# Block 2 in half products, batch 3's attention one block earlier, and the sums and squares moved with them

## The chip, the cores and the metric

The kernel runs on one NeuronCore of one Trainium2 chip. The metric is the device time of one execution in microseconds (us). Its engines are TensorE (PE), VectorE (DVE), ScalarE (ACT), GpSimd (POOL) and SyncE (SP), whose queue here issues the transposing DMAs and the stores.

## The reference

```python
kv  = einsum('bhsd,bhse->bhde', k, v)          # q, k, v: [8, 8, 576, 64] fp32
o   = einsum('bhsd,bhde->bhse', q, kv)
att = o / sqrt(mean(o*o, -1) + 1e-6) * g_norm
x   = att.transpose(0, 2, 1, 3).reshape(4608, 512)
ffn = (gelu(x @ w_gate) * (x @ w_val)) @ w_out   # 512 -> 1536 -> 512
out = x + sigmoid(x @ w_res) * ffn
```

## The kernel before

A block is the 512 first tokens of one batch (blocks 0 to 7). The 64 last tokens of the eight batches together make block 8. TensorE runs, for each block: 12 slices of gate and value products (512 columns each), four gate products `rps`, then the product with w_out as seven products of half size instead of eight. In some blocks the gate and value products, too, are done as half products: a *group* of four slices takes 2 x 7 x 4 matmuls of 256 columns in place of 2 x 4 x 4 of 512. They need sums of weights and of tokens, made by DVE.

The attention of a later batch is woven into the block's slots, one slot being one slice or one step of the products. Each batch needs: q brought to token order by copies (`by_token`), a DMA transpose `d_qT`, the k-v product (`a_kv`), the o product (`a_o`, which reads qT), squares on ACT and reductions on DVE (`a_ss`), a normalisation of about a dozen tiny operations (`a_norm`), the scaled result t (`a_t`), its multiplication by g (`a_x`), and a DMA transpose `d_xT` for the matmuls. The program puts each engine's work into its queue in this order, so a slot number is a place in five queues.

Names in the trace lines: `gps` and `vps` are a slice's gate and value products, `hid` is DVE's product of the two (it frees their banks of PSUM), `op` the o product, `rps` the four gate products with w_res, `wA`, `wD`, `wE` and `wF` the banks of the seven products with w_out. The *F sum* is DVE's addition that makes `wF`, which a later product needs, and the *half sums* are sums of `hid` for these products. `osb` holds the block's result; a *residual addition* is POOL's addition of x (`t`) to it.

```python
    def plan_attn(b):                  # batches 2 and 3
        ...
        if b == 2:
            at(m, 0, lambda: by_token(b))
            at(m, 1, *begin)           # begin: attn_begin, d_qT, last tokens' transpose
            k0, o0, n0 = 4, 6, 9
        else:
            if b == 3:
                aside_out(m - 1, "22", lambda: by_token(b), *begin)
            ...
            k0, o0, n0 = 1, 3, 7
        at(m, k0, lambda: a_kv(b))
        ...
        at(m, NF, lambda: d_xT(b, 0, NJ))
        ...
    GROUPS = {blk: (1, 2) for blk in range(3, B - 1)} | {B - 1: (1, 0, 2), B: (0, 1, 2)}
    ...
    def plan_attn_ahead(b):            # batches 4 to 7, two blocks ahead
        ...
        else:                          # m, the block it runs in, is not in GROUPS
            at(m, 5, lambda: by_token(b, act, slice(0, 2)))
            at(m, 6, lambda: by_token(b, act, slice(2, 4)))
            at(m, 7, *begin)
            at(m, NF - 1, lambda: a_kv(b, act))
            at(m, NF, lambda: load_behind(b, b - 1))
        ...
        at(m, NF, lambda: a_o(b), lambda: a_ss(b, 0), lambda: a_ss(b, 1))
        aside_out(m, "D", lambda: a_ss(b, 2), lambda: a_ss(b, 3))
        aside_out(m, "gates", *[lambda: a_ss(b, NJ)] * rem, lambda: a_norm(b, 0, NJ + rem, pool))
```

## Time and profile before

| | before |
|---|---|
| time, median of runs (lowest to highest) | 333.25 us (333.08 to 333.75) |
| span of the profiled run, granted clock | 331.3 us, 0.995 |
| PE, DVE, ACT, POOL busy | 97%, 78%, 56%, 40% |
| blocks 1, 2, 3, 4 | 35.91, 37.24, 35.19, 33.45 us |
| blocks 5, 6, 7 | 34.46, 32.12, 30.96 us |

A block's length is the start of its first gate matmul in the TensorE timeline taken from that of the next block. The share of busy time hides the stages: with TensorE at 97%, what counts is which block has a gap, and whose work ends it. The lines are shown in the prediction.

### The profile page before, as it was taken

To read this page: it belongs to the slowest core of one execution; us is meant where nothing else is said; L and a number is where in the kernel's file an instruction comes from. 1 tells how busy PE (TensorE), PEld (TensorE's weight loads), DVE (VectorE), ACT (ScalarE), POOL (GpSimd) and SP (SyncE) were. 2 spreads that over 40 slices of the span, in tenths; PEclk is the share of its full clock that TensorE was granted. 3 is DMA by queue.
4 is the path that set the end of the run, shared out by engine and by line. 5 is a ranking of instruction groups with operands and counts; after the bars stand their busy time and mean duration, and the time that the engine had idled before them with its cause. 6 is when DMAs were issued, how large, how long until landed. Compare 5 with 4: busy or idle time off the path is not lost.

```text
span 331.3 us, 7035 instructions
## 1 busy us (share of the span) xinstructions
PE 320.6 (97%) x2768; PEld 219.6 (66%) x2768; DVE 258.7 (78%) x482; ACT 184.6 (56%) x334; POOL 133.9 (40%) x196
## 2 busy tenths in 40 slices
PE   8899999999999999899999999999999999999993
PEld 3554454445844476686768686868587888788882
DVE  6856769579867996869786987697979977687754
ACT  3763474374338381667466746675465466646660
POOL 2882152980055038418641864114611241151232
PEclk9999999999999999999999999999999999999997
DMA  8999999679579749976937593800340030011004
GB/s 256 318 205 203 195 203 177 161 120 136 85 126 202 156 72 162 223 110 77 141 137 136 66 150 129 143 4 0 129 79 3 0 129 3 0 64 64 2 0 127
DMA packets 76690, 38.85 MB, mean 117 GB/s; under 512 B 42098, under 2 KB 74354, under 8 KB 76658
## 3 DMA queue, kind: packets, MB, share of 16 engines
q0 software_dynamic: 38752, 17.17, 41.3%
q1 hardware_dynamic: 37328, 20.71, 24.3%
q10 hardware_dynamic: 578, 0.52, 0.5%
q8 instruction: 21, 0.34, 0.4%
q14 instruction: 11, 0.09, 0.1%
HBM read 38.80 MB, written 9.44 MB: 146 GB/s over the span
## 4 chain that ended last, share of the span: by engine, by line
PE 88%; DVE 4%; DMA 3%; SPq 1%; ACT 1%; issue 1%; POOL 0%; DVEq 0%; ACTq 0%
PE vps L361 13%; PE gps L361 13%; PE rps L381 10%; PE wA L456 9%; PE Av L698 8%; PE Ag L698 7%; PE Fv L698 4%; PE Fg L698 4%; PE fps L398 3%; PE w L456 2%; PE wD L456 2%; PE wF L456 2%; PE wE L456 2%; PE Ev L698 2%; PE Eg L698 2%; PE kvp L208 2%
## 5 line engine op out<-in xcount | busy, mean ns | idle before, releaser
L349 ACT ACTIVATE ge<-gps 128x512 f16<-128x512 f32 x52 | 30.8, 597 | 64.6 <-PE gps L361 64.3
L361 PE MATMUL vps<-xT,wv 128*128 128x512 f16 x200 | 51.3, 379 | 0.9 <-DVE hid L350 0.9
L361 PE MATMUL gps<-xT,wg 128*128 128x512 f16 x200 | 51.4, 379 | 0.3 <-DMA xT<-t 0.3
L350 DVE TENSOR_TENSOR hid<-ge,vps 128x512 f16<-128x512 f16 x52 | 35.4, 683 | 20.0 <-PE vps L361 17.5
L698 PEld LDWEIGHTS <-ws 128*128 128x128 f16 x448 | 43.6, 98 | 5.6 <-issue 0.5
L735 POOL TENSOR_TENSOR hid<-ge,c 128x512 f16<-128x512 f16 x14 | 16.3, 1163 | 73.1 <-ACT ge L729 73.1
L456 PEld LDWEIGHTS <-hid_s 128*128 128x128 f16 x384 | 37.5, 98 | 6.1 <-issue 1.7
L498 POOL TENSOR_TENSOR osb<-osb,t 128x512 f32<-128x512 f32 x28 | 32.0, 1168 | 23.0 <-DVE osb L494 22.7
L361 PEld LDWEIGHTS <-wv 128*128 128x128 f16 x200 | 19.6, 98 | 24.6 <-issue 1.1
L361 PEld LDWEIGHTS <-wg 128*128 128x128 f16 x200 | 19.0, 98 | 21.8 <-DMA xT<-t 0.6
L381 PE MATMUL rps<-wr,xT 128*128 128x512 f16 x144 | 33.3, 380 | 0.0
L456 PEld LDWEIGHTS <-hid 128*128 128x128 f16 x288 | 28.1, 98 | 5.4 <-issue 0.4
L390 ACT ACTIVATE th<-rps 128x512 f32<-128x512 f32 x36 | 21.5, 598 | 12.2 <-PE rps L381 12.2
L381 PEld LDWEIGHTS <-xT 128*128 128x128 f16 x144 | 13.5, 98 | 14.8
L719 DVE TENSOR_TENSOR Fg<-Ag,d 128x512 f32<-128x512 f32 x14 | 9.8, 700 | 16.2 <-PE Ag L698 9.0
L245 DVE TENSOR_REDUCE ss<-sq 128x8 f32<-128x512 f32 x32 | 20.6, 678 | 2.3 <-ACT sq L243 1.9
L456 PE MATMUL wA<-wo_ts,hid_s 128*128 128x256 f16 x168 | 20.6, 272 | 1.0 <-DVE wF L429 1.0
L307 DVE TENSOR_TENSOR t<-op,ny 128x512 f16<-128x512 f32 x28 | 18.2, 684 | 2.8 <-POOL ny L287 2.7
L395 ACT ACTIVATE th<-th 128x512 f32<-128x512 f32 x36 | 19.9, 625 | 0.0
L698 PEld LDWEIGHTS <-wg 128*128 128x128 f16 x168 | 16.4, 98 | 2.7
L698 PEld LDWEIGHTS <-wv 128*128 128x128 f16 x168 | 16.4, 98 | 1.9
L698 PE MATMUL Ag<-ts,ws 128*128 128x256 f16 x112 | 16.8, 273 | 0.0
(183 smaller groups left out, 649.5 us busy)
## 6 DMA issues: line engine op xcount, KB each, us to landing
out_dram<-osb SPq DMA_DIRECT2D x14, 512.0 KB, 2.7
qraw<-in_q_dram POOLq DMA_DIRECT2D x7, 512.0 KB, 6.7
k<-in_k_dram POOLq DMA_DIRECT2D x7, 512.0 KB, 8.4
v<-in_v_dram POOLq DMA_DIRECT2D x7, 512.0 KB, 11.4
wg<-in_moe_w_gate_dram POOLq DMA_DIRECT2D x2, 512.0 KB, 8.1
wv<-in_moe_w_val_dram POOLq DMA_DIRECT2D x2, 512.0 KB, 8.7
wo<-in_moe_w_out_dram POOLq DMA_DIRECT2D x2, 512.0 KB, 13.8
out_dram<-osb SPq DMA_DIRECT2D x4, 256.0 KB, 2.7
```

Source lines behind the costliest of these rows:

```text
L245: nc.vector.tensor_reduce(out=out_, in_=sq, op=ALU.add, axis=mybir.AxisListType.X)
L307: nc.vector.tensor_tensor(out=t, in0=o, in1=scale, op=ALU.mult)
L349: nc.scalar.activation(out=ge, in_=gps, func=AF.Gelu)
L350: nc.vector.tensor_tensor(out=hids[blk][:, f, :], in0=ge, in1=vps, op=ALU.mult)
L361: nc.tensor.matmul(ps[:, j0 * P : j1 * P], lhsT=w[:, cc, :], rhs=xT_t[blk][:, j0:j1, cc, :], start=(cc == 0 and j0 == 0), stop=(cc == NP - ...
L381: nc.tensor.matmul(rps, lhsT=xT_t[blk][:, j, cc, :], rhs=wr16[:, cc, :], start=(cc == 0), stop=(cc == NP - 1),)
L390: nc.scalar.activation(out=th, in_=rps, func=AF.Tanh, scale=0.5)
L395: nc.scalar.activation(out=th, in_=th, func=AF.Copy, scale=0.5, bias=0.5)
L456: nc.tensor.matmul(ps[:, e - es[0], :], lhsT=a[:, f, e * P : (e + 1) * P], rhs=b[:, f, :], start=(start and e == es[0] and f == 0), stop=( ...
L498: nc.gpsimd.tensor_tensor(out=res_all[of], in0=res_all[of], in1=t_t[blk][of], op=ALU.add)
L698: nc.tensor.matmul(out_[:, r, :], lhsT=lhsT, rhs=rhs, start=(first and r == 0 and c == 0), stop=(c == 1), skip_group_check=True,)
L735: eng.tensor_tensor(out=dst, in0=ge[q], in1=source(q, "v"), op=ALU.mult)
```

## The change

Its intent: half products in block 2 save TensorE time. They are affordable only if batch 3's attention leaves block 2, so it moves to block 1. Block 1's DVE and POOL work is rearranged to make room.

```diff
+    def plan_attn_2():
+        b, m = 2, 1
+        act = nc.scalar.copy
+        at(m - 1, 2 * NF + 3, lambda: by_token(b, act, slice(0, 2)))
+        at(m, 0, lambda: by_token(b, act, slice(2, 4)), lambda: attn_begin(b), lambda: d_qT(b))
+        at(m, 2, lambda: a_kv(b))
+        at(m, 3, lambda: load_behind(b))
+        at(m, 1, lambda: wo_sums(1))          # all sums of w_out on DVE now
+        at(m, 3, lambda: wo_sums(3))
+        at(m, 4, lambda: a_o(b))
         ...
+        at(m, 6, lambda: a_norm(b, 0, NJ))
+        for j in range(NJ):
+            at(m, 7 + j // 2, lambda j=j: a_t(b, j))
+            at(m, 8 + j // 2, lambda j=j: a_x(b, j))
+        at(m, 9, lambda: d_xT(b, 0, NJ))
-    GROUPS = {blk: (1, 2) for blk in range(3, B - 1)} | ...
+    GROUPS = {blk: (1, 2) for blk in range(2, B - 1)} | ...
     # plan_attn_ahead, now for batches 3 to 7; block 1 is the only one not in GROUPS
-            at(m, 5, lambda: by_token(b, act, slice(0, 2)))
-            at(m, 6, lambda: by_token(b, act, slice(2, 4)))
-            at(m, 7, *begin)
+            at(m, 9, lambda: by_token(b, act, slice(0, 2)))
+            at(m, 10, lambda: by_token(b, act, slice(2, 4)), *begin)
-            at_word(m, 1, "h21", lambda: a_rem_o(b))
-        at(m, NF, lambda: a_o(b), lambda: a_ss(b, 0), lambda: a_ss(b, 1))
+            at_word(m, 1, "h21", lambda: a_rem_o(b), lambda: a_sq(b, NJ))   # square at once
+        at(m, NF, lambda: a_o(b), *[lambda: a_red(b, NJ)] * rem, lambda: a_ss(b, 0), lambda: a_ss(b, 1))
-        aside_out(m, "gates", *[lambda: a_ss(b, NJ)] * rem, lambda: a_norm(b, 0, NJ + rem, pool))
+        aside_out(m, "F", lambda: a_norm(b, 0, NJ + rem, pool))
     # last tokens: two batches' worth each with batches 4, 5, 6, 7 (before: 2, 3, 5, 7)
-        return b // 2 if b % 2 == 1 and b > 1 else 0 if b == 2 else None
+        return b - B // 2 if b >= B // 2 else None
     # token sums always between the w_out products; block 1's residual additions sooner
-            at(blk + 1, 5, lambda: fin((0, 0)))       # and 6, 9, 10
+            at(blk + 1, 0, lambda: fin((0, 0)))       # and 1, 2, 3
     # batch 1's four multiplications by g: from block 2's first slots to the end of block 1
    # cut: third hidden sum later, late weight sums spread over block 6, buffer counts and banks,
    # the xT wait in front of a batch's loads, last tokens' xT in the next block's first group
```

More of the change, by code (lines that the diff above doesn't have):

```diff
@@ L123, in load_batch @@
         load_last_kv(b)
-        for i in {2: (0, 1), 3: (2, 3)}.get(b, (b,) if b > 1 else ()):
-            load_qr(i)
+        if pair(b) is not None:
+            load_qr(2 * pair(b))
+            load_qr(2 * pair(b) + 1)
     def by_token(b, copy=nc.vector.tensor_copy, js=slice(0, NJ)):
@@ L171, in attn_begin @@
             "kv2": (
-                attnp.tile([P, NP, D], FP16, tag="kv2", bufs=3, name="kv2")
+                attnp.tile([P, NP, D], FP16, tag="kv2", bufs=4, name="kv2")
                 if b > 0
@@ L237, in of_o, with a_sq, a_red @@
         return ap[:, 2 * jj : 2 * jj + 2].rearrange("p j (r e) -> p j r e", e=2)[:, :, :, e]
-    def a_ss(b, i):
-        o, ss = st[b]["o"][i], st[b]["ss"]
-        sq = attnp.tile([P, 2, NP, D] if i < NJ else [P, H, D], FP32, tag="sq", name="sq")
-        src = o if i < NJ else o.rearrange("p (h d) -> p h d", h=H)
-        nc.scalar.activation(out=sq, in_=src, func=AF.Square)
-        out_ = of_o(ss, i) if i < NJ else ss[:, NJ, :]
-        nc.vector.tensor_reduce(out=out_, in_=sq, op=ALU.add, axis=mybir.AxisListType.X)
+    sqs = {}
+    def a_sq(b, i):
+        o = st[b]["o"][i]
+        sqs[b, i] = attnp.tile([P, 2, NP, D] if i < NJ else [P, H, D], FP32, tag="sq", bufs=3, name="sq")
+        src = o if i < NJ else o.rearrange("p (h d) -> p h d", h=H)
+        nc.scalar.activation(out=sqs[b, i], in_=src, func=AF.Square)
+    def a_red(b, i):
+        ss = st[b]["ss"]
+        out_ = of_o(ss, i) if i < NJ else ss[:, NJ, :]
+        nc.vector.tensor_reduce(out=out_, in_=sqs.pop((b, i)), op=ALU.add, axis=mybir.AxisListType.X)
+    def a_ss(b, i):
+        a_sq(b, i)
+        a_red(b, i)
     def a_rem_o(b):
@@ L433, in wo_sums @@
         pairs = [(b_of(1, 2), b_of(1, 1)), (b_of(2, 2), wo_t[:, 0]), (b_of(2, 2), b_of(1, 2)), (b_of(2, 1), wo_t[:, 1])]
-        if i in (0, 2):
-            sub(nc.vector, wo_t[:, i], *pairs[i])
-            return
-        for f in range(0, NFH, 2):
-            sub(nc.gpsimd, wo_t[:, i, f : f + 2, :], *(x[:, f : f + 2, :] for x in pairs[i]))
+        sub(nc.vector, wo_t[:, i], *pairs[i])
     def s_begin(blk):
@@ L449, in s_rest, with s_last @@
         sub(nc.vector, s_[1], s_[0], a_of(blk, 1, 1))
-        sub(nc.vector, s_[3], a_of(blk, 1, 2), s_[1])
+    def s_last(blk):
+        sub(nc.vector, hid_sums[3], a_of(blk, 1, 2), hid_sums[1])
     def prod(ps, a, b, start, es=(0, 1)):
@@ L480, in first_two @@
             w["d"] = finp.tile([P, 2, CH], FP32, tag="wd", bufs=1, name="wd")
+            s_last(blk)
             prod(w["A"], a_of(blk, 1, 1), b_of(1, 1), True)
@@ L536, in out_by_products @@
         if later:
-            at(blk + 1, 5, lambda: fin((0, 0)))
-            at(blk + 1, 6, lambda: fin((0, 1)), lambda: store(0))
-            at(blk + 1, 9, lambda: fin((1, 0)))
-            at(blk + 1, 10, lambda: fin((1, 1)), lambda: store(1))
+            at(blk + 1, 0, lambda: fin((0, 0)))
+            at(blk + 1, 1, lambda: fin((0, 1)), lambda: store(0))
+            at(blk + 1, 2, lambda: fin((1, 0)))
+            at(blk + 1, 3, lambda: fin((1, 1)), lambda: store(1))
         return [lambda: res(0), lambda: res(1), first_two, others]
@@ L569, in run @@
             d = finp.tile([P, 2, CH], FP32, tag="wd", bufs=1, name="wd")
-            u = attnp.tile([P, 2, CH], FP32, tag="sq", name="u")
+            u = attnp.tile([P, 2, CH], FP32, tag="sq", bufs=3, name="u")
             one = (slice(0, 1), slice(1, 2))
+            s_last(blk)
             for e in range(2):
@@ L710, in keep @@
         def keep(u):
-            sb["d", u] = attnp.tile([P, 2, PR], FP32, tag="sq", name="d")
+            sb["d", u] = attnp.tile([P, 2, PR], FP32, tag="sq", bufs=3, name="d")
             nc.scalar.copy(out=sb["d", u], in_=ps["F", u])
@@ L941, in f_sq @@
     def f_sq(pr, j0, j1):
-        first["sq", pr, j0] = sq = attnp.tile([P, j1 - j0, 2, D], FP32, tag="sq", name="sq")
+        first["sq", pr, j0] = sq = attnp.tile([P, j1 - j0, 2, D], FP32, tag="sq", bufs=3, name="sq")
         ps = first["o", pr].rearrange("p j (h d) -> p j h d", h=2)
@@ L1106, in aside_out @@
         amid_out.setdefault(blk, {}).setdefault(ahead_of, []).extend(fs)
-    def plan_attn(b):
-        rem = pair(b) is not None
-        m = b - 1
-        begin = [lambda: attn_begin(b), lambda: d_qT(b)]
-        if rem:
-            begin.append(lambda: d_rem_qT(b))
-        if b == 2:
-            at(m, 0, lambda: by_token(b))
-            at(m, 1, *begin)
-            k0, o0, n0 = 4, 6, 9
-        else:
-            if b == 3:
-                aside_out(m - 1, "22", lambda: by_token(b), *begin)
-            else:
-                at(m - 1, NF, lambda: by_token(b))
-                at(m - 1, NF + 1, *begin)
-            k0, o0, n0 = 1, 3, 7
-        at(m, k0, lambda: a_kv(b))
-        if b + 1 < B:
-            at(m, k0 + 1, lambda: load_behind(b))
-        if rem:
-            at(m, o0 - 1, lambda: a_rem_o(b))
-            at(m, o0 + 2, lambda: a_ss(b, NJ))
-        at(m, o0, lambda: a_o(b))
+    def plan_attn_2():
[8 more added lines that the diff above has]
+        at(m, 4, lambda: a_o(b))
@@ L1134, in plan_attn @@
         for j in range(NJ):
-            at(m, o0 + j // 2, lambda j=j: a_ss(b, j))
-        at(m, n0, lambda: a_norm(b, 0, NJ + rem))
-        n0 += 1 if b == 2 else 2
+            at(m, 4 + j // 2, lambda j=j: a_ss(b, j))
+        at(m, 6, lambda: a_norm(b, 0, NJ))
         for j in range(NJ):
-            at(m, NF if b == 2 and j > 1 else n0 + j // 2, lambda j=j: a_t(b, j))
-        for j in range(NJ):
-            at(m, NF if b == 2 else n0 + 1, lambda j=j: a_x(b, j))
-        at(m, NF, lambda: d_xT(b, 0, NJ))
@@ L1143, in plan_attn @@
-        last = [lambda: a_t(b, NJ), lambda: a_x(b, NJ), lambda: d_xT(b, NJ, NJ + 1)]
-        if rem and m + 1 in GROUPS:
-            aside_out(m, "F", *last)
-        elif rem:
-            at(m, NF + 3, *last)
-    GROUPS = {blk: (1, 2) for blk in range(3, B - 1)} | {B - 1: (1, 0, 2), B: (0, 1, 2)}
+            at(m, 7 + j // 2, lambda j=j: a_t(b, j))
+            at(m, 8 + j // 2, lambda j=j: a_x(b, j))
+        at(m, 9, lambda: d_xT(b, 0, NJ))
+    GROUPS = {blk: (1, 2) for blk in range(2, B - 1)} | {B - 1: (1, 0, 2), B: (0, 1, 2)}
@@ L1170, in plan_attn_ahead @@
         else:
-            at(m, 5, lambda: by_token(b, act, slice(0, 2)))
-            at(m, 6, lambda: by_token(b, act, slice(2, 4)))
-            at(m, 7, *begin)
+            at(m, 9, lambda: by_token(b, act, slice(0, 2)))
+            at(m, 10, lambda: by_token(b, act, slice(2, 4)), *begin)
             at(m, NF - 1, lambda: a_kv(b, act))
-            at(m, NF, lambda: load_behind(b, b - 1))
+            at(m, NF, lambda: load_behind(b))
         if rem:
-            at_word(m, 1, "h21", lambda: a_rem_o(b))
-        at(m, NF, lambda: a_o(b), lambda: a_ss(b, 0), lambda: a_ss(b, 1))
+            at_word(m, 1, "h21", lambda: a_rem_o(b), lambda: a_sq(b, NJ))
+        at(m, NF, lambda: a_o(b), *[lambda: a_red(b, NJ)] * rem, lambda: a_ss(b, 0), lambda: a_ss(b, 1))
         aside_out(m, "D", lambda: a_ss(b, 2), lambda: a_ss(b, 3))
-        aside_out(m, "gates", *[lambda: a_ss(b, NJ)] * rem, lambda: a_norm(b, 0, NJ + rem, pool))
+        aside_out(m, "F", lambda: a_norm(b, 0, NJ + rem, pool))
         at(m, NF + 3, lambda: new_block(b), lambda: a_t(b, 0), lambda: a_t(b, 1))
@@ L1187, in plan_attn_ahead @@
         if rem:
-            at(m + 1, 3, lambda: a_x(b, NJ), lambda: d_xT(b, NJ, NJ + 1))
+            at_word(m + 1, 0, "h21", lambda: a_x(b, NJ), lambda: d_xT(b, NJ, NJ + 1))
     units = [(n, g) for g in (1, 2, 0) for n in "gv"]
@@ L1195 @@
     late_sums = [f for u in (("g", 0), ("v", 0)) for f in sums[u]]
-    at(B - 2, NF + 1, *late_sums[0:4])
-    for key, f in zip(("00", "22", "01", "11"), late_sums[4:8]):
-        aside_out(B - 2, key, f)
+    for i, f in enumerate(late_sums[0:4]):
+        at_word(B - 2, i // 2, ("Fv", "h21")[i % 2], f)
+    at(B - 2, NF + 1, *late_sums[4:8])
     for blk in GROUPS:
         t = token_sums(blk, nc.vector)
-        if blk - 1 in GROUPS and blk < B:
-            at(blk - 1, NF + 1, *t)
-        else:
-            for key, f in zip(("00", "01", "22", "11"), t):
-                aside_out(blk - 1, key, f)
+        for key, f in zip(("00", "22", "01", "11"), t):
+            aside_out(blk - 1, key, f)
     out_at = {}
@@ L1249 @@
             slots += outs
-            for b in range(2, B):
-                (plan_attn if b - 1 not in GROUPS else plan_attn_ahead)(b)
+            plan_attn_2()
+            for b in range(3, B):
+                plan_attn_ahead(b)
             plan[5] = [lambda j=j: a_x(0, j) for j in range(NJ)]
@@ L1275, in banks_ahead @@
                     att_at[blk] = list(pattn.turn)
-                    pattn.opening = [pattn.turn[0]] + pattn.turn
+                    pattn.opening = pattn.turn[2:3] + pattn.turn
                 plan.setdefault(NF - 2, []).append(banks_ahead)
@@ L1280 @@
                 slots[0] = lambda: m_gval(1, 0, pattn, "at")
-                plan.setdefault(3, []).append(lambda: (wo_sums(1), wo_sums(3)))
             outs = []
@@ L1299 @@
             late = []
-            if blk == 2:
-                for j, g in enumerate(rows):
-                    plan.setdefault(j, []).append(g)
+            if blk == 1:
+                plan.setdefault(NF + 3, [])[0:0] = rows
         if blk == 0:
```

## The prediction

> **What bounds the kernel now.** I read the busy table and the chain's totals, then the windows block by block, then the TensorE timeline for its gaps, and last VectorE (DVE), ScalarE (ACT), GpSimd (POOL) and the transposing DMA queue (SP) around each gap.
>
> ```profile
> PE 320.6 (97%) x2768; PEld 219.6 (66%) x2768; DVE 258.7 (78%) x482; ACT 184.6 (56%) x334; POOL 133.9 (40%) x196
> ...
> PE 88%; DVE 4%; DMA 3%; SPq 1%; ACT 1%; issue 1%; POOL 0%; DVEq 0%; ACTq 0%
> ```
>
> TensorE is busy 97% of the span and owns 88% of the chain that ended last: a change pays only by taking matmuls away or closing a TensorE gap. The windows of blocks 1 to 5, each from its first matmul to the next block's (columns: window, length, busy time of PE, weight loads, DVE, ACT, POOL, clock, DMA):
>
> ```profile
> 55.30:91.20 35.90, 35.56 (x285) 20.27 (x283) 28.60 (x54) 16.06 (x29) 17.34 (x19) 1.00 0.87 127
> 91.20:128.50 37.30, 36.98 (x357) 21.50 (x358) 31.24 (x64) 20.15 (x36) 16.39 (x26) 1.00 0.89 142
> 128.50:163.65 35.15, 34.09 (x335) 25.02 (x333) 27.57 (x46) 21.89 (x40) 18.83 (x37) 1.00 1.05 146
> 163.65:197.10 33.45, 33.45 (x319) 24.93 (x317) 27.74 (x47) 20.62 (x37) 16.87 (x30) 1.00 0.71 120
> 197.10:231.55 34.45, 33.96 (x334) 25.04 (x332) 27.67 (x46) 21.90 (x40) 10.96 (x21) 1.00 0.31 68
> ```
>
> Block 4 is what a block with half products costs when nothing waits and no last tokens are in it: 33.45 us. Blocks 3 and 5 are longer by waits and by last tokens, block 2 because it does no half products and carries two batches' attention. The gaps in the TensorE timeline:
>
> ```profile
> 91.22 1.04 PE L361 MATMUL gps<-xT,wg 128*128 128x512 f16 x4 [0.33 <-DMA xT<-t]
> ...
> 124.54 1.47 PE L456 MATMUL wA<-wo_ts,hid_s 128*128 128x256 f16 x12 [0.30 <-DVE wF L429]
> ...
> 133.80 1.02 PE L361 MATMUL vps<-xT,wv 128*128 128x512 f16 x4 [0.86 <-DVE hid L350]
> ...
> 159.72 1.47 PE L456 MATMUL wA<-wo_ts,hid_s 128*128 128x256 f16 x12 [0.20 <-DVE wF L429]
> ...
> 227.63 1.47 PE L456 MATMUL wA<-wo_ts,hid_s 128*128 128x256 f16 x12 [0.49 <-DVE wF L429]
> ...
> 262.37 1.47 PE L456 MATMUL wA<-wo_ts,hid 128*128 128x256 f16 x12 [0.19 <-DVE osb L429]
> ```
>
> The brackets are less than the loss, since the modelled end of a matmul overlaps the next start. Counted by cadence (from 122.76, twelve matmuls of 0.109 us would end at 124.07, so 124.54 is 0.47 late) they cost 0.50, 0.47, 1.02, 0.36, 0.66 and 0.36 us. Some 0.15 us gaps come on top. So perhaps 4 us are to be had from waits.
>
> **What the Trainium skill says.** "TensorE: Matmul & The Clock Gate", section "Wait — 56ns, not 53.3ns?": a warm matmul of N columns starts N / 2.4 GHz + about 2.5 ns after the last, 215.7 ns for 512. The trace agrees: four take 0.86 us, and twelve of 256 take 1.31 us. The same page, section "Architectural detail: the array is 16× 32×32, not 1× 128×128": VectorE and ScalarE are strict FIFO; TensorE pulls only weight loads ahead. The trace agrees: the matmul at 133.80 waited for a product queued on DVE behind normalisations. "DMA: Bandwidth & Descriptors", section "DMA Transpose (X-bar)": the plain transpose is issued only from Sync or Scalar. Here all are on the one SP queue, and they stand one behind the other:
>
> ```profile
> 86.28 1.70 SPq L338 DMA_TRANSPOSE xT<-t  x1
> 88.40 3.31 SPq L325 DMA_TRANSPOSE qT<-q  x1
> ...
> 93.12 0.18 POOL L1095 COPY hold<-qT 1x1 f16<-1x1 f16 x1 [19.76 <-DMA qT<-q]
> ```
>
> The reader is to see the second issue begin after the first, and POOL released at 93.12, 4.7 us after the qT issue began.
>
> **The change part by part.**
>
> Half products in block 2: two groups of four slices. A group takes 2 x 4 x 4 = 32 matmuls of 512 columns now, and 2 x 7 x 4 = 56 of 256 then, worth 28. Two groups save 8 x 0.216 = 1.73 us. All of it is on the path.
>
> Attention of batch 3 moves from block 2 to block 1: 40 kv matmuls (0.86 us with their gap) and 32 o matmuls (0.67). TensorE sum zero. The last tokens move too: 16 matmuls, 0.35 with gap, leave blocks 1 and 3's schedule for batches 4 to 7, done in blocks 2 to 5: block 1 −0.35, block 4 +0.35, others as before. Sum zero.
>
> Sums of w_out: six POOL additions of 1.23 us (7.2) become two on DVE of about 0.9 each (the row of the other two: 0.95). Off the path, but they free POOL at 59, so batch 3's loads start at about 63 instead of 68.
>
> Squares at once, token sums after the F sum, third hidden sum later: in blocks 3 and 5 five reductions (about 3.0 us) and four token sums (1.4) stood before the F sum. Taking 1.4 and the late last-token reduction (0.6) from in front brings F ahead of need: gaps 0.47, 0.36, 0.66 close. xT of batch 2 is asked for in slot 9 of block 1, before its end, so 0.50 closes. In block 3 the 1.02 wait came from POOL's normalisation, late behind loads; loads now go out earlier, so it closes. Block 6's late weight sums are spread: 0.36 closes.
>
> Block 1 is the hard place, for DVE. I follow its queue from starts and intervals in the trace: hid 0.60, half sum 0.87, normalisation 2.41, two t 1.19, multiplication by g 0.33. Block 1 starts at 55.31 as before; slices are 1.73 apart, kv of batch 2 falls after slice 2, o after slice 4 at 64.9. Reductions end at 69.2. Then: hid of slice 6 from 69.3, normalisation to 72.3, hid 7 to 72.9, two t to 74.1, hid 8 to 74.7, half sum to 75.6, two t to 76.8, two by g to 77.4, hid 9 to 78.05, two by g to 78.7. The second matmul group of slice 11 could start at 76.8 but reuses the bank of hid 9: 1.35 us lost. The xT transpose of batch 2 is issued at 78.85, its issue takes 1.9, so that of qT of batch 3 begins at 80.85 and lands at 85.6. Its own copies on ACT end at 76.9, so SP is what holds it. TensorE, with kv of batch 3 and the first half of the gate products done, reaches o of batch 3 at 81.7: it waits 3.9 us. Block 2 then starts at 97.2, not at the 91.73 that its matmuls alone give (35.24 bare − 0.35 + 1.53 from 55.31) and not at today's 91.22.
>
> From there: block 2 takes 33.45 + 0.35 = 33.8, ends 131.0 (today 128.46, +2.5). Block 3 33.8 for 35.19: +1.1. Block 4 33.8 for 33.45: +1.5. Block 5 33.8 for 34.46: +0.8. Block 6 31.75 for 32.12: +0.45. Blocks 7 and 8 alike. Sum: 333.37 + 0.45 = 333.8 us.
>
> **The rivals.** First: the new wait is small. My DVE queue may be late, or the loads and transposes may land sooner; then all gaps close, and 1.73 + about 3 us fall, 329 to 330. For it speaks that slots look tuned (copies split over slots 9 and 10); against it that old block 2 had these copies four slots earlier, ended at 106.4, qT landed at 111.8 and was used at 116.5: four slots are 6.9 us, more than the 4.7 of slack, without xT in front.
>
> Second: the wait is as I say, and the clock suffers too. The same TensorE page, section "What's actually happening", gives 3.4 us of idle as able to halve the clock. 3.9 us could, if it covers a whole window: 1 to 2 us more, 335 to 336. The trace has no such idle after the opening.
>
> Third: v of batch 3 comes late for kv in slot 11. Issue at about 65 plus 11.5 (median) is 76.5, maximum seen 14, 79; kv is due at 79. This would hide in the qT wait.
>
> Fourth: the POOL bound in block 2, where four residual additions (1.15 each) move to its first slots behind a normalisation; DVE has 0.4 us of slack there, so up to half a us.
>
> **Range and chances.** The mechanism weighs about two thirds (333.8, give or take one), the first rival one third (330). Between them I put 333.0 us, range 329.6 to 335.4. Either way it is inside 2% (326.7 to 340.0): faster 0.02, same 0.96, slower 0.02.
>
> **What would show it.** The half products: 64 fewer matmuls of 512 columns and 112 more of 256, block 2 near 33.8. The wait: a TensorE gap of 3 to 4 us before o in block 1, released by DMA qT, with SP's qT issue directly behind xT; if that gap is under 1 us I am wrong and the first rival holds. A 1.35 us gap at slice 11's second group released by hid. The F gaps of blocks 3 and 5 gone. Wrong altogether: a new gap in blocks 2 to 5, from POOL's normalisation or the banks.

## The result and the profile after

| | before | after |
|---|---|---|
| time, median (lowest to highest) | 333.25 (333.08 to 333.75) | 336.44 (335.77 to 337.12) |
| span of the profiled run, clock | 331.3, 0.995 | 334.0, 0.991 |
| block 1 | 35.91 | 43.42 |
| block 2 | 37.24 | 34.75 |
| block 3 | 35.19 | 33.80 |
| block 4 | 33.45 | 33.80 |
| block 5 | 34.46 | 33.81 |
| block 6 | 32.12 | 31.75 |
| block 7 | 30.96 | 30.97 |

The change is 0.93% slower: ratio 1.0093, 95% interval 1.0068 to 1.0119. A ratio here is the mean time of one kernel's fast runs over that of the other's of the same rounds, so not quite the ratio of the medians. All runs quoted are in the fast state. The opening of a profiled run varies by up to 0.8 us between kernels that do the same there, so I compare lengths of blocks, not absolute times.

Blocks 2 to 6 together are 4.55 us shorter, as meant (172.46 us before, 167.91 after). The count of matmuls rose from 2768 to 2816: 64 fewer and 112 more, as predicted. Block 1 is 7.51 us longer. Its matmuls at full clock and without a gap would take 36.42 us (an estimate from the prediction's rows: 35.24 bare before, less 0.36 of last tokens, plus 1.54 of batch 3), so 7.00 of its 43.42 us are waits and clock. The TensorE timeline of the changed kernel (start, length, engine, line, operation, in brackets the idle time before it and what ended it) has four lines that tell where these are, and where block 2 lost time:

```profile
77.86 1.02 PE L371 MATMUL vps<-xT,wv 128*128 128x512 f16 x4 [1.20 <-DVE hid L360]
...
85.35 0.83 PE L227 MATMUL op<-kv,qT 64*128 64x64 f16 x32 [3.88 <-DMA qT<-q]
86.11 3.33 PE L391 MATMUL rps<-wr,xT 128*128 128x512 f16 x8
...
103.80 1.02 PE L371 MATMUL vps<-xT,wv 128*128 128x512 f16 x4 [0.79 <-DVE hid L360]
```

The first and second are the two gaps in block 1. The third has no bracket, no gap at all, and is yet wrong: the same eight matmuls take 1.90 us elsewhere. The windows around it say why (columns: window, length, busy PE, weight loads, DVE, ACT, POOL, then granted clock, DMA share, GB/s):

```profile
81.40:85.35 3.95, 0.07 (x2) 0.01 (x2) 0.27 (x1) 0.60 (x1) 0.00 (x0) 1.00 0.95 177
85.35:86.11 0.76, 0.76 (x32) 0.67 (x33) 0.00 (x0) 0.32 (x1) 0.32 (x2) 0.69 0.00 0
86.11:89.28 3.17, 3.17 (x12) 1.14 (x9) 2.15 (x3) 1.36 (x3) 3.17 (x4) 0.54 0.56 56
89.28:90.59 1.31, 1.31 (x13) 1.17 (x12) 0.00 (x0) 0.60 (x1) 1.31 (x3) 1.00 1.43 195
```

After 3.95 us in which TensorE did nothing, the granted clock is 0.69 and then 0.54 for about four microseconds, then 1.00 again. A busy TensorE is not a fast one: this loss shows in the busy column as work.

The transposing queue of the changed kernel shows the two issues one behind the other:

```profile
78.54 1.84 SPq L348 DMA_TRANSPOSE xT<-t  x1
80.48 2.58 SPq L335 DMA_TRANSPOSE qT<-q  x1
```

The copies that qT waits for ended on ACT at 76.5, but qT is asked for only at 80.48 and releases TensorE at 85.35, 4.87 us later.

For the fourth line, DVE's timeline at the start of block 2 in the changed kernel:

```profile
99.58 2.38 DVE L331 TENSOR_TENSOR t<-t,g 128x512 f16<-128x512 f16 x4
```

and POOL's:

```profile
100.40 4.79 POOL L507 TENSOR_TENSOR osb<-osb,t 128x512 f32<-128x512 f32 x4 [1.24 <-DVE t L331]
```

Four multiplications by g in a row took 1.42 us in the kernel before (at 84.71 and 115.28). Here they take 2.38, and POOL's residual additions, each of which needs such a product as its `t`, start in the middle of them. The product that frees a bank stands behind them in DVE's queue.

### The profile page after: what moved, and what is told of

It is laid out like the page before. It is cut to its first block, busy times and chain, and to the rows that moved or that the text cites. A ratio compares the mean times of both kernels' runs of the same rounds, so it can differ in the third digit from the quotient of the medians.

```text
span 334.0 us, 7160 instructions
## 1 busy us (share of the span) xinstructions
PE 319.9 (96%) x2816; PEld 224.7 (67%) x2816; DVE 259.9 (78%) x479; ACT 191.8 (57%) x347; POOL 138.5 (41%) x206
## 4 chain that ended last, share of the span: by engine, by line
PE 86%; DVE 7%; DMA 3%; SPq 1%; issue 1%; POOL 0%; DVEq 0%
PE wA L464 11%; PE rps L391 10%; PE vps L371 9%; PE gps L371 9%; PE Av L708 9%; PE Ag L708 8%; PE Fv L708 4%; PE Fg L708 4%; PE fps L408 3%; PE wF L464 3%; PE wE L464 3%; PE wD L464 3%; PE w L464 2%; PE Eg L708 2%; PE Ev L708 2%; PE kvp L209 2%
## 5 line engine op out<-in xcount | busy, mean ns | idle before, releaser
L359 ACT ACTIVATE ge<-gps 128x512 f16<-128x512 f32 x44 | 26.1, 597 | 55.8 <-PE gps L371 55.7
L745 POOL TENSOR_TENSOR hid<-ge,c 128x512 f16<-128x512 f16 x16 | 18.6, 1164 | 86.1 <-ACT ge L739 86.1
L708 PEld LDWEIGHTS <-ws 128*128 128x128 f16 x512 | 49.7, 98 | 6.6 <-issue 0.7
L371 PE MATMUL vps<-xT,wv 128*128 128x512 f16 x168 | 43.1, 379 | 2.0 <-DVE hid L360 2.0
L371 PE MATMUL gps<-xT,wg 128*128 128x512 f16 x168 | 43.2, 380 | 0.0
L360 DVE TENSOR_TENSOR hid<-ge,vps 128x512 f16<-128x512 f16 x44 | 29.8, 683 | 12.4 <-PE vps L371 9.9
L391 PE MATMUL rps<-wr,xT 128*128 128x512 f16 x144 | 34.9, 392 | 0.0
L729 DVE TENSOR_TENSOR Fg<-Ag,d 128x512 f32<-128x512 f32 x16 | 11.2, 700 | 18.3 <-PE Ag L708 9.7
L708 PE MATMUL Ag<-ts,ws 128*128 128x256 f16 x128 | 19.3, 273 | 0.0
L708 PE MATMUL Av<-ts,ws 128*128 128x256 f16 x128 | 19.2, 273 | 0.0
```

The costliest lines, as they stand in the source:

```text
L359: nc.scalar.activation(out=ge, in_=gps, func=AF.Gelu)
L360: nc.vector.tensor_tensor(out=hids[blk][:, f, :], in0=ge, in1=vps, op=ALU.mult)
L371: nc.tensor.matmul(ps[:, j0 * P : j1 * P], lhsT=w[:, cc, :], rhs=xT_t[blk][:, j0:j1, cc, :], start=(cc == 0 and j0 == 0), stop=(cc == NP - ...
L391: nc.tensor.matmul(rps, lhsT=xT_t[blk][:, j, cc, :], rhs=wr16[:, cc, :], start=(cc == 0), stop=(cc == NP - 1),)
L708: nc.tensor.matmul(out_[:, r, :], lhsT=lhsT, rhs=rhs, start=(first and r == 0 and c == 0), stop=(c == 1), skip_group_check=True,)
L729: nc.vector.tensor_tensor(out=dst, in0=ps["A", u], in1=sb["d", u], op=ALU.add)
```

## The experiments

My theory after this: the time is lost in block 1 to qT's place in the queue behind xT, to the clock that the wait brings down, and in block 2 to POOL running beside DVE. All other parts of the change do what they should. The rivals are named with each run. Times of the kernel before, run beside them, were 333.09 us (runs 1 to 4), 333.72 (5 to 8) and 333.21 (9).

**1. The order of the two transposes swapped.**

```diff
-        at(m, 9, lambda: d_xT(b, 0, NJ))                       # plan_attn_2
-            at(m, 10, lambda: by_token(b, act, slice(2, 4)), *begin)
+            at(m, 10, lambda: by_token(b, act, slice(2, 4)), *begin, lambda: d_xT(b - 1, 0, NJ))
```

> Only the order of two transposes in block 1 is swapped: qT of batch 3 is asked for before xT of batch 2. Theory (qT waits behind xT in the one SP queue, and the long idle slows TensorE's clock): qT's issue begins at about 76.6 instead of 80.5, as soon as its copies on ACT end, lands at about 81.5, the gap before o of batch 3 falls from 3.88 us to under 0.6, the clock stays at 1.00, and the time falls by about 5 us from 336.4 to 331 to 332. Rival (the late ACT copies, or the transpose itself, set the wait): the gap stays at 3 us or more and the time within 1 us of 336.4.

Measured: 331.01 us (330.69 to 331.05), ratio to before 0.9933 (0.9918 to 0.9948). The SP queue of this run, whose block 1 began 0.8 us later (55.91 for 55.11):

```profile
77.33 1.83 SPq L335 DMA_TRANSPOSE qT<-q  x1
79.31 2.46 SPq L348 DMA_TRANSPOSE xT<-t  x1
```

Its TensorE timeline at the o matmuls of batch 3:

```profile
82.20 0.64 PE L227 MATMUL op<-kv,qT 64*128 64x64 f16 x32
82.78 1.90 PE L391 MATMUL rps<-wr,xT 128*128 128x512 f16 x8
```

No bracket before the o matmuls: the gap is gone, and the eight gate matmuls are at 1.90 again. One line of program order was worth 5.4 us, and the change with it is faster than the kernel before. The theory held, the rival fell. The two hid gaps (1.20 and 0.79) stayed as they were.

**2. The copies earlier, the queue unchanged.**

```diff
-            at(m, 9, lambda: by_token(b, act, slice(0, 2)))
-            at(m, 10, lambda: by_token(b, act, slice(2, 4)), *begin)
+            at(m, 7, lambda: by_token(b, act, slice(0, 2)))
+            at(m, 8, lambda: by_token(b, act, slice(2, 4)))
+            at(m, 10, *begin)
```

> Only the two ACT copies that feed qT of batch 3 are moved two slots earlier (7 and 8 for 9 and 10), the transposes keep their order. Theory (queue order): no change, gap 3.5 to 4 us, 335.5 to 337. Rival (the copies are what is late): the gap shrinks by about 3.5 us and the time falls to about 332.

Measured: 336.43 us (335.88 to 337.71). The TensorE timeline at the o matmuls:

```profile
85.39 0.64 PE L227 MATMUL op<-kv,qT 64*128 64x64 f16 x32 [3.88 <-DMA qT<-q]
```

The gap is 3.88 us, as in the changed kernel; block 1 is 43.47. What fed qT was ready two slots sooner (the copies on ACT end at 73.1 for 76.5) and nothing moved. It was the queue.

**3. TensorE kept busy in the wait.**

```diff
+    def warm_wait():
+        w = pmoe.tile([P, C], FP32, name="idle2", bank=out_at[1][2])
+        for _ in range(15):
+            nc.tensor.matmul(w, lhsT=zeros[:, 0:P], rhs=zeros, start=True, stop=True)
...
+        if b == 3:
+            at(m, NF, lambda: warm_wait())
         at(m, NF, lambda: a_o(b), ...)
```

> 15 matmuls of zeros (512 columns, result unused) are put before o of batch 3, so that TensorE is busy for about 3.2 us of the wait and the wait itself stays. Theory (idle lowers the granted clock): the gap before o shrinks to under 1 us, the eight gate matmuls behind it last about 1.9 us instead of 3.33, clock 0.995 instead of 0.991, the time falls by 1.3 to 1.7 us to about 335. Rival (those matmuls were slow for another reason, such as POOL's loads starting just then): they last 3.3 us again and the time stays at 336.4.

Measured: 335.44 us (335.23 to 335.69), clock 0.998 in the profiled run. Its TensorE timeline:

```profile
81.34 3.40 PE L1181 MATMUL idle<-zeros 128*128 128x512 f16 x15
86.53 0.64 PE L227 MATMUL op<-kv,qT 64*128 64x64 f16 x32 [1.78 <-DMA qT<-q]
87.10 1.90 PE L391 MATMUL rps<-wr,xT 128*128 128x512 f16 x8
```

The eight gate matmuls last 1.90 us: the clock is what had slowed them, and idling is what had slowed the clock. The gain is 1.0 us, not 1.3 to 1.7, and the gap is 1.78, not under 1: in this profile qT landed 6.05 us after its issue began (80.48 to 86.53) against 4.87 without the dummies. Why, I did not find out; the issue itself took 3.84 us instead of 2.58. Both lie within what transposes of this kind show elsewhere (issues of 1.4 to 4.9 us over all runs; in the kernel before, landing 4.3 to 6.5 us after the issue began). The runs of this kernel and of the first lie within 0.5 us of each other; those of the changed kernel spread over 1.35, and its two slower runs had the lower clock (0.987 against 0.991 and 0.992). That the penalty varies from run to run is thus likely. The four profiles that have this wait do not settle it: from the first o matmul to the end of the gate products they show 3.93 us (the change), 3.96 (run 2), 3.58 (run 4) and 3.94 (run 9), against 2.31 in run 1.

**4. The residual additions put back.**

```diff
-            at(blk + 1, 0, lambda: fin((0, 0)))        # and 1, 2, 3
+            at(blk + 1, 5, lambda: fin((0, 0)))        # and 6, 9, 10
```

> Only the residual additions of block 1 on POOL go back from slots 0 to 3 of block 2 to slots 5, 6, 9 and 10. Theory (they slow the four multiplications by g on DVE, 2.38 us for about 1.35, which delays the product that frees a bank): the gap of 0.79 us at slice 2 of block 2 vanishes, the time falls by 0.8 to 1.0 us to about 335.5. Rival (the late normalisation on POOL sets it): the gap stays above 0.5 us and the time within 0.4 us of 336.4.

Measured: 342.87 us (341.27 to 343.55), slower by 6.4 us. This expectation failed, in an instructive way. From the DVE timeline of this run:

```profile
99.74 1.42 DVE L331 TENSOR_TENSOR t<-t,g 128x512 f16<-128x512 f16 x4
```

That is as expected: without POOL beside them the multiplications take 1.42 us again, and the gap of 0.79 is gone. So the mechanism was right. But the TensorE timeline has a new gap at the end of block 2:

```profile
135.78 2.13 PE L464 MATMUL wA<-wo_ts,hid 128*128 128x256 f16 x12 [4.43 <-DVE osb L439]
```

In block 2 slot 9 no longer means what it did: a whole group fills slot 8, so slots 9 and 10 come behind both groups. The last two additions of block 1 stood in POOL's queue behind the seven loads of the next batch and ran at 126.21; their store was issued at 128.59 and, among those loads, took 6.3 us to land, to 134.9. DVE must not overwrite that part of the result before the store has read it: it began at 135.03 after 5.18 us, and TensorE behind it. (The profile puts DVE's wait down to a POOL addition that ended at the same moment. That one belongs to block 2 and comes later in the program, so the store is the likelier cause.) The clock fell again behind this gap, to 0.67 and then 0.50 for 3.6 us. The residual additions had to move; only slots 0 to 3 were a poor place for them.

**5. The three gaps mended together.**

```diff
-            at(m, 9, lambda: by_token(b, act, slice(0, 2)))
-            at(m, 10, lambda: by_token(b, act, slice(2, 4)), *begin)
+            at(m, 7, lambda: by_token(b, act, slice(0, 2)))
+            at(m, 8, lambda: by_token(b, act, slice(2, 4)), *begin)
-                plan.setdefault(NFH + 2, []).insert(0, lambda: s_begin(blk))
+                plan.setdefault(NF + 1, []).append(lambda: s_begin(blk))
-            at(blk + 1, 0, lambda: fin((0, 0)))        # and 1, 2, 3
+            at(blk + 1, 5, lambda: fin((0, 0)))        # and 5, 6, 6: between the two groups
```

> The changed kernel with its three gaps mended: copies and qT of batch 3 in slots 7 and 8 (so qT stands ahead of xT in the queue), the first half sum of block 1 moved from slot 8 to behind the gate products, and block 1's residual additions on POOL put between the two groups of half products of block 2 (not behind both, as in the run that put them back). Theory: no TensorE gap over 0.3 us between 25 and 320 us; 331.0 of the queue swap less 1.35 less 0.96 is 328.7, so 328 to 329.5, below both kernels. Rival (there is a further limit, DVE or POOL, that takes over once the gaps close): a new gap, 330 us or more.

Measured: 328.69 us (328.56 to 329.20), ratio to before 0.9859 (0.9844 to 0.9873), clock 1.000. Blocks 1 to 7 take 37.00, 33.81, 33.80, 33.80, 33.80, 31.76 and 30.96. The only TensorE wait left between 25 and 320 us, in its timeline, is this one, 0.03 over what I had allowed:

```profile
77.13 1.02 PE L371 MATMUL vps<-xT,wv 128*128 128x512 f16 x4 [0.33 <-DVE hid L360]
```

This version beats both kernels: 7.75 us under the change as given, 1.4% under the kernel before.

**6. The half products of block 2 undone, all else as in 5.**

```diff
-    GROUPS = {blk: (1, 2) for blk in range(2, B - 1)} | ...
+    GROUPS = {blk: (1, 2) for blk in range(3, B - 1)} | ...
-        if rem:
+        if rem and m in GROUPS:
             at_word(m, 1, "h21", lambda: a_rem_o(b), lambda: a_sq(b, NJ))
+        elif rem:                      # last tokens in a block without groups
+            at(m, NF - 1, lambda: a_rem_o(b), lambda: a_sq(b, NJ))
     # cut: the order of the banks, fitted to this; block 2 does not open block 3's buffers
```

> As the mended kernel, but block 2 computes all twelve slices whole, as before the change: the half products of block 2 undone alone. Theory: block 2 is longer by 2 x (6.91 less 6.12) = 1.6 us, the time 1.6 us over the mended kernel, 330 to 331. Rival (the half products cost as much in waits on DVE and ACT as they save): within 0.5 us of the mended kernel, or faster.

Measured: 331.50 us (331.31 to 332.07), 2.8 us over the mended kernel; 1.6 was expected. Block 2 is 36.38 for 33.81, 2.57 us longer. Whole slices account for 1.58: four take 6.91 us (8 x 0.864), a group 6.12 in the windows of the changed kernel. The rest, 0.99, is two waits that this form brings with it, 0.56 us on a DVE product and 0.46 on the copy of kv that last tokens read at once. The run's other 0.25 us lie in block 8 of its profile; why, I don't know. So this run gives an upper bound for the half products, and 1.58 is their own part by count and cadence. They save less than the 1.73 that I had put because I took a matmul of 256 columns as half of one of 512: a group is 56 at 0.1092 us, not at 0.108.

**7. Two sums of w_out back on POOL, all else as in 5.**

```diff
-        sub(nc.vector, wo_t[:, i], *pairs[i])
+        if i in (0, 2):
+            sub(nc.vector, wo_t[:, i], *pairs[i])
+            return
+        for f in range(0, NFH, 2):
+            sub(nc.gpsimd, wo_t[:, i, f : f + 2, :], *(x[:, f : f + 2, :] for x in pairs[i]))
```

> As the mended kernel, but two of the four sums of w_out are back on POOL (six additions, 7.2 us). Theory: POOL can ask for batch 3's data only at about 66 to 67 instead of 62.7, q lands at 73.5 or later, the ACT copies wait up to 3 us for it and the gelus behind them too, kv of batch 3 waits for v: 2 to 3 us over the mended kernel. Rival (the loads have slack, so the sums' engine does not matter): within 0.5 us of it.

Measured: 329.84 us (329.65 to 330.29), 1.15 us over the mended kernel, all of it in block 1 (38.15 for 37.00). Neither side was right. The loads were not late (the first was asked for at 63.05): the second sum falls behind them in the queue. It ran to 70.5 and pushed POOL's last residual addition behind it, so that both ran beside DVE's normalisation. On POOL:

```profile
67.10 3.42 POOL L439 TENSOR_TENSOR wo_ts<-wo,wo_ts 128x512 f16<-128x512 f16 x3
70.45 1.18 POOL L419 TENSOR_TENSOR osb<-osb,t 128x512 f32<-128x512 f32 x1
```

On DVE:

```profile
70.05 0.52 DVE L285 TENSOR_SCALAR nm<-ss 128x32 f32<-128x32 f32 x1
70.60 1.07 DVE L286 TENSOR_SCALAR ny<-nm 128x32 int32<-128x32 int32 x1
```

In the mended kernel both take 0.18. The first stands beside the end of the sum, the second beside the addition and ends with it; together they are 1.23 us longer. DVE then runs late to the end of the slices, and two gaps of 0.77 and 0.58 us stand where one of 0.33 did. The sums on DVE do pay here, and the trace shows POOL beside DVE as the cause, not the loads.

**8. Square and reduction of the last tokens late again, all else as in 5.**

```diff
-            at_word(m, 1, "h21", lambda: a_rem_o(b), lambda: a_sq(b, NJ))
+            at_word(m, 1, "h21", lambda: a_rem_o(b))
-        aside_out(m, "F", lambda: a_norm(b, 0, NJ + rem, pool))
+        aside_out(m, "gates", *[lambda: a_ss(b, NJ)] * rem, lambda: a_norm(b, 0, NJ + rem, pool))
```

> As the mended kernel, but the square and reduction of the last tokens stand again late, behind the D product, with the normalisation behind them. Theory: the sum F comes late by 0.2 to 0.4 us in each of blocks 3 to 5 and 2, about 1 us in all over the mended kernel. Rival (moving the token sums behind F was enough): within 0.4 us of it.

Measured: 329.79 us (329.46 to 331.17), 1.1 us over the mended kernel. Blocks 2 to 5 take 34.07, 34.06, 34.07 and 34.07 for 33.80, which is 0.27 each and 1.07 together. DVE's timeline in block 3 shows the late reduction directly in front of the F sum, which in the mended kernel waits for nothing but TensorE there:

```profile
156.00 0.69 DVE L251 TENSOR_REDUCE ss<-sq 128x8 f32<-128x512 f32 x1 [0.21 <-ACT sq L246]
156.60 0.69 DVE L439 TENSOR_TENSOR wF<-wA,wd 128x512 f32<-128x512 f32 x1
```

As expected: square and reduction at once are worth a quarter of a microsecond in each block with last tokens. (The edit moves POOL's normalisation too, which has to wait for the reduction; its share is not separated. The profiled run, slower than the median by 0.8 us, also has a block 1 longer by 0.28, in its k-v product, which the edit does not touch.)

**9. The half sum of block 1 late, nothing else, on the change as given.**

```diff
-                plan.setdefault(NFH + 2, []).insert(0, lambda: s_begin(blk))
+                plan.setdefault(NF + 1, []).append(lambda: s_begin(blk))
```

> The changed kernel with only the first half sum of block 1 moved from slot 8 on DVE to behind the gate products. Theory (what sets o of batch 3 is the chain DVE, xT issue, qT issue, landing; TensorE's 1.2 us gap at slice 11 lies inside that wait): the gap at slice 11 falls to about 0.3 us, and the gap before o changes by the difference: xT is issued 0.9 us earlier (77.7), qT lands near 84.4, TensorE reaches o 0.9 to 1.0 us earlier, so the gap before o stays near 3.9 and the time falls by 0.9 us or so to about 335.5; the clock penalty stays. Rival (the two gaps are independent, TensorE's own gap is all that matters): the same fall with the gap before o smaller by more than 0.5 us, or no fall at all.

Measured: 335.64 us (335.04 to 336.03), 0.8 us under the change. The SP queue:

```profile
78.32 1.84 SPq L348 DMA_TRANSPOSE xT<-t  x1
80.26 2.60 SPq L335 DMA_TRANSPOSE qT<-q  x1
```

The o matmuls in the TensorE timeline:

```profile
85.12 0.77 PE L227 MATMUL op<-kv,qT 64*128 64x64 f16 x32 [3.87 <-DMA qT<-q]
```

Block 1 began 0.65 us later in this profile (55.76 for 55.11), so xT was asked for 0.87 earlier within it. The gap at slice 11 fell to 0.32 us, block 1 to 42.54 (0.88 less), and the gap before o stayed at 3.87. Both TensorE and the chain that it waits for start from DVE's queue, so relieving DVE moves both by the same amount and leaves the wait as long as it was. The theory named this; the rival asked for a smaller gap.

## Why the prediction was wrong

The prediction named each wait, and nearly all its sizes came out. The time lay above its range, because two terms were left out of its sum, and because it gave a third of the weight to a case that did not happen.

- *Bound.* TensorE sets the time: right. Every difference of block lengths above is a TensorE gap, a matmul count, or the clock.
- *Half products.* Put at 1.73 us, they are 1.58 by count and cadence. The saving is real and lies on the path: undoing them alone cost 2.57 us in block 2, two new waits included.
- *Gaps to close.* The F gaps of blocks 2, 3 and 5, the xT wait at block 2 and the wait in block 3 are gone. Blocks 3, 4 and 5 were put at 33.8 each and measure 33.80, 33.80 and 33.81; block 6 at 31.75 and measures 31.75. The run with late squares shows one of the causes alone; the others (token sums behind F, earlier loads, the earlier xT, the weight sums of block 6) were not undone one by one.
- *Block 1, DVE.* The queue worked through by hand gave 1.35 us lost at slice 11; it is 1.36 (77.86 where 76.50 was due by cadence). SP's qT issue came directly behind xT, as said.
- *Block 1, wait.* "It waits 3.9 us": 3.88. Swapping the transposes removed it, moving the copies did not.
- *The step that failed.* "Block 2 then starts at 97.2" makes block 1 41.89 us long. It was 43.42. The difference of 1.53 is the clock, which the second rival held at "1 to 2 us more" and the sum held at nothing: from the o matmuls to the end of the gate products took 3.93 us (85.35 to 89.28), against 2.31 in the run with the swapped transposes (82.20 to 84.51), so 1.62 us. The busy wait undid it. A predicted wait of 3.9 us, against the 3.4 that the prediction quoted, should have been in the sum, not beside it.
- *The second term.* "Block 2 takes 33.45 + 0.35": it took 34.75, with a gap of 0.96 by cadence. The fourth rival had the place (POOL's additions at the start of block 2) and allowed half a microsecond. It missed that these additions also lengthen DVE's multiplications, by 0.96 us. The prediction's own sign of being "wrong altogether", a new gap in blocks 2 to 5, thus came in block 2, from POOL's additions and not from its normalisation.
- *The third rival* (v late for kv of batch 3) did not come: TensorE has no wait before that product.
- *The sum.* 333.8 with 1.53 and 0.95 is 336.3, and the median is 336.44. That they agree to 0.1 is partly luck: both terms are from the profiled run, the fastest of the four, at 335.77.
- *The weights.* The first rival, that the author had tuned the slots and the wait would be small, pulled the number to 333.0 on no line of the profile. The prediction had itself the line against it (the same copies four slots earlier left 4.7 us of slack, and the change took away 6.9).
- *w_out's sums.* "They free POOL at 59, so batch 3's loads start at about 63": they did, at 62.66, but that was not what paid (run 7).

## What to carry to other kernels

When work moves to an earlier stage, follow each DMA that it issues back to the queue it stands in, and ask what is in front of it: a transpose that is ready can wait behind one that is not. If a wait on TensorE comes near four microseconds, add the slow clock behind it to the sum (3.9 and 4.4 us brought it down, the 1.8 us of the busy wait did not; nothing between was measured). A slot number is worth what stands in the slots around it: when a stage changes shape, go through everything that was placed there by number.

## What the Trainium skill lacked or had wrong

- "DMA: Bandwidth & Descriptors", section "DMA Transpose (X-bar)", gives constraints, and the page elsewhere an effective bandwidth for transposes, but not how long the issue of one holds its queue. Here the issue of a 128 x 2048 fp16 transpose (qT) from SP held the queue for 1.4 to 4.9 us over all runs (2.58 in block 1 of the changed kernel), and qT landed 4.3 to 6.5 us after its issue began in the kernel before. Of two in a row, the second landed 6.8 us (78.54 to 85.35) after the first's issue began.
- "Advanced Engine Details and Errata", section "X-Bar Transpose (TRN2)", says that transposes are as fast as regular DMAs. In the kernel before, the qT transposes (512 KB) landed in a median of 5.3 us and the xT transposes (512 KB, but four of the ten smaller) in 4.3, a plain store of 512 KB in 2.7. The stores go to memory and the transposes do not, and the loads of 512 KB from POOL took longer (q 6.7, v 11.4), so this does not show the page wrong.
- "SBUF — State Buffer", section "Who interferes with whom", says that a DVE instruction with two SBUF inputs contends with a GpSimd instruction that reads SBUF. The trace agrees and adds a size: four multiplications of 128 x 512 fp16, with two inputs each, took 2.38 us beside POOL's additions, 1.42 without. A DVE operation on 128 x 32 numbers with a single input was slowed too, which that sentence does not cover: 1.07 us beside one addition, 0.18 without (run 7).
- "TensorE: Matmul & The Clock Gate", section "What's actually happening", says that the clock halves after an idle window of about 3.4 us, and the trace agrees: after 3.95 us idle the granted clock was 0.69 and then 0.54 for 3.9 us in all. It lacks the remark that such time is shown as busy: only the clock and the length of a known group of matmuls (3.33 us for 1.90) give it away.
